# Two units of an attention, expert and gated chain with eight block products instead of seven

## The chip, the cores and the metric

One core of one Trainium2 chip runs the whole program. The metric is the device time of one execution in microseconds (us). TensorE (PE) does the matrix products and reads its stationary operand through a second row, PEld. VectorE (DVE), ScalarE (ACT) and GpSimd (POOL) do the elementwise work, SyncE (SP) issues the DMAs.

## The reference, cut to what matters

```python
x = attention(q, k, v)                   # 1152 tokens x 512
P = balanced_gates(x @ w_gate)           # 1152 x 8, eight rounds of scaling
out = sum(P[:, e:e+1] * (relu(x @ w1[e]) @ w2[e]) for e in range(8))   # 8 experts, 1024 wide
a, b = out @ w_a, out @ w_b              # 1536 wide
return (a * b) @ w_out
```

All of it is in float32, and the weights w_a, w_b and w_out come as 64-bit floats.

## The kernel before, in words

Each float32 operand is split into a high and a low part (ACT casts the high part, DVE or POOL subtracts it from the raw number for the low one, lines 130 to 140), and each product is done as three matmuls, high by high, high by low and low by high (lines 59, 60).

Half an expert (512 hidden columns) is a unit: units 0 and 1 are expert 0, unit 2 is the first half of expert 1, and so on to unit 15. After them come six gated units of 256 hidden columns each (`glu_g`), which multiply a by b instead of taking the maximum with zero. Units 0 and 1 run while the attention still runs, over blocks of 384 tokens.

From unit 2 on, the 1152 tokens are done in two chunks of 512 and 640 (`CN`, half a chunk is 256 or 320 tokens). Each of the two is a `phase`: the hidden layer of one unit and chunk (`g_chunk`), with the output tiles of the unit and chunk before (`o_tile`, 12 matmuls of 512 columns, 6 in a gated unit) put between its products at `PLACES`. The hidden layer is a product of 2 by 2 blocks, done with seven block products (A11, S2, S1, A12, S3, A22, S4) where eight are the plain way. Each block product is two groups of six matmuls. In return, sums have to be made: of weight blocks (`queue_combined`, seven blocks a unit, most of it on POOL) and of token blocks (`combine_x`: four totals on line 573, four differences on line 581, casts on line 587, low parts on line 594). The token sums T1 to T4 are made once for each chunk before unit 2, and again before the first gated unit, since there the tokens are the experts' output, transposed by `t_step`. T1 is written over a part of the tokens' own tiles `xh` and `xl`.

The program is written out in one order, and each engine keeps the order in which its instructions are emitted. What is emitted between the products is set by a small model of the engines' times (`Model`, `pump`, `force`): tasks stand in the queues `tq` (token sums), `wq` (weight splits) and `dq` (decoding of the 64-bit weights), and `pump` takes one when the model says that its engine has room. The decoding is 48 pieces through two buffers: load, an absolute value on ACT, seven instructions on DVE, an addition on POOL, and a store to DRAM (lines 330 to 402). What is left of it is run before unit 15 (lines 1319, 1320). PSUM gives six banks to hidden groups, and two to output tiles.

Steps of the change and of the prediction touch these lines: `queue_plain` 235, `queue_combined` 247, `combine_x` 541, `g_chunk` 616, `phase` 720, `close_attention` 1171, the end of units 0 and 1 at 1267 to 1278, unit 2 at 1304 to 1314, the first gated unit at 1331 to 1360.

Of the kernel before, what the change touches and what calls it, by code (L numbers as in the profile page):

```python
# [19 lines left out]
def attn_moe_glu_kernel(  # L20
# [16 lines left out]
    nc = tc.nc  # L37
# [21 lines left out]
    def mm(o, l, r, start, stop, check=True):  # L59
        nc.tensor.matmul(out=o, lhsT=l, rhs=r, start=start, stop=stop, skip_group_check=not check)  # L60
# [94 lines left out]
    def run(q):  # L155
        t = q.pop(0)
        t.fn()
        return t
# [14 lines left out]
    def force(cond):  # L173
        while not cond():
            if not (wq and (not wq[0].slot or slot_free() or RING[nring[0] % NSLOT].uses == 0)):
                raise RuntimeError("nothing left to prepare")
            run(wq)
# [54 lines left out]
        lq.extend(rs)  # L232
        return rs

    def queue_plain(u):

        u.w = {}
        rs = halves(u.load1, (2, 2))
        for i in range(2):
            for j in range(2):  # L240
                def piece(i=i, j=j):
                    b = u.w[i, j] = new_block(NB * 2)
# [373 lines left out]
    def g_chunk(u, c, glu=False):  # L616
# [44 lines left out]
        for a, b, bk in PRODUCTS:  # L661
# [46 lines left out]
                finish(0, 0, 0, G4[:, :n], True)  # L708
            yield


    PLACES = {5: (1, 2, 3, 4, 5), 4: (1, 3, 4, 5), 3: (1, 4, 5)}

# [5 lines left out]

    def phase(u, c, tiles, glu=False, places=None):  # L720

        places = places or PLACES[len(tiles)]
        for i, _ in enumerate(g_chunk(u, c, glu)):
            gate_step()
            for t, at in zip(tiles, places):
                if at == i:
                    t()
                    gate_step()
# [382 lines left out]
    with tc.manual_schedule():  # L1111
# [29 lines left out]
            queue_plain(u)  # L1141
        for u in units[:2]:
            queue_out(u)
        queue_combined(units[2], nc.gpsimd)
        extra = []

        def spare_block(uses):
# [21 lines left out]
                n -= run(wq).slot  # L1169

        def close_attention():
            nonlocal closed, ps3, Th, Tl, tmp_p
# [7 lines left out]
            tmp_p = tmp_stack.enter_context(tc.tile_pool(name="tmp", bufs=1, side="right"))  # L1180
            ps3 = ctx.enter_context(tc.tile_pool(name="ps3", bufs=6, space=PSUM))
            gens[0] = gating()
            v, g = nc.vector, nc.gpsimd
            tasks = combine_x(0, lambda name: tmp_p.tile([128, 2, CN[0]], F32, name=name),
                              (v, g, g, v), (g, g, g, g))
            tq.extend(tasks[:-2])
            late.extend(tasks[-2:])
            queue_out(units[2])
            for u in units[3:]:
                queue_combined(u)  # L1190
                queue_out(u)
            for u in glu_g:
                queue_combined(u)
                queue_out(u, 2)
            hold[0] = False
            for r in coming:
                r.tile
            fetch()
# [12 lines left out]
                else:  # L1211
                    close_attention()

        Th = Tl = tmp_p = G4 = None
        G3, late = [], []
        tmp_stack = ExitStack()
        turn = 0.0
        nside = 0

# [15 lines left out]
        for b in range(NB):  # L1235
            while ready[0] < b:
                side_step()
                if b == 0:
                    warm(WARM[1])
                nside += 1  # L1240
                if nside > 12 and nside % 2 == 0:
                    run_first(1)
            if b == NB - 1:
                while not closed:
                    side_step()
                M.dve = M.act = M.pe
# [8 lines left out]
            if b == NB - 1:  # L1255
                tq.extend(late)
            per = TB // 128
            firsts = [[
                lambda n=n, t=t, b=b: o_moe(
                    units[n], *([G[n][:, f] for f in range(4)] for G in GP), t, b * per + t, mid)  # L1260
                for t in range(per)
            ] for n in range(2)]
            for n in range(2 if b < NB - 1 else 1):
                for t in firsts[n]:
                    t()
                    step()
        while tq:
            run(tq)
        M.dve, M.act, M.pool = min(M.dve, M.pe + 1), min(M.act, M.pe + 1), min(M.pool, M.pe + 1)
        tmp_stack.close()  # L1270
        g0p = ctx.enter_context(tc.tile_pool(name="g0p", bufs=1, side="right"))
        t1 = {}
        for x, names in (("gh0", ("t1", "b12")), ("gl0", ("b22", "b21"))):
            t = gp.tile([128, 1536], F32, tag=x, name=f"t{x}")
            for i, name in enumerate(names):
                t1[name] = t[:, i * 640:(i + 1) * 640].rearrange("p (k n) -> p k n", k=2)
        v, g = nc.vector, nc.gpsimd
        tq.extend(combine_x(1, lambda name: t1[name], (v, g, g, v), (g, g, g, g)))
# [52 lines left out]
        def transposed(c, part=None):  # L1331
            x0, x1 = keep[c]
            where = {"t1": x0[:, 0:2], "b12": x1[:, 0:2], "b22": x1[:, 2:4], "b21": x0[:, 2:4]}
            tq.extend(combine_x(c, lambda name: where[name], (v, g, g, v), None, part))

        for t, tt in enumerate(TILES[1]):
            o_tile(units[last], 1, t)
            if t == 0:
                steps = [t_step(t0, keep) for t0 in TILES[0]]
                for _ in range(2):  # L1340
                    for x in steps:
                        next(x, None)
                transposed(0)
            else:
                for _ in t_step(TILES[1][t - 1], keep):
                    pass
                if t == 4:
                    transposed(1, slice(0, 192))
        while tq:
            run(tq)  # L1350
# [9 lines left out]
        phase(glu_g[0], 1, o_tiles(glu_g[0], 0), True)  # L1360
# [35 lines left out]
```

## Time and profile before

| What | us |
|---|---|
| three runs, median | 1136.14 |
| lowest and highest of the three | 1133.69, 1141.28 |
| the profiled execution | 1141.77 |
| its span, from the first to the last instruction | 1140.0 |

The profiled execution lies 5.6 us above the median. Its mean granted clock is 0.974. Times of rows are counted from the start of the span. PEclk is the granted clock of TensorE as a share of 2.4 GHz (1.00 in text), 0.50 is 1.2 GHz.

### The profile page before, as it was taken

Reading aid. Unit: us, or ns where it says so; the run is one execution under the profiler, and the core shown is the slowest. Engines: PE = TensorE matmul, PEld = TensorE weight load, DVE = VectorE, ACT = ScalarE, POOL = GpSimd, SP = SyncE. Lnnn points to the kernel's source line nnn. Section 1 sums busy time; section 2 is a strip of 40 time slices with the busy share of each in tenths; the row PEclk is TensorE's granted clock in tenths of the full one; section 3 lists DMA queues with packets and bytes.
Section 4 is the critical chain, followed back from the end, with each engine's and each line's share of the span. In section 5 each row is a group of like instructions: output and inputs, shape, how many; then the busy total and the mean of one; then the engine's idle time right before and its main releaser. Section 6 shows DMA issues by size and latency. Waiting matters only on the chain.

```text
span 1140.0 us, 18222 instructions
## 1 busy us (share of the span) xinstructions
PE 1097.3 (96%) x6545; PEld 994.1 (87%) x6545; DVE 804.1 (71%) x1593; ACT 459.0 (40%) x1203; POOL 541.6 (48%) x540
## 2 busy tenths in 40 slices
PE   8998999979999999999999999999999979999998
PEld 6897898768889999899998999989899778999997
DVE  6566453777878878778787788877754665666764
ACT  5555442344344443444434444344443532323321
POOL 3312312475355464554645646456453334546431
PEclk9599999989999999999999999999999989999999
DMA  6243200112322323323233132331310101011102
GB/s 168 52 130 101 65 16 1 38 66 65 100 97 75 118 71 120 99 66 118 85 114 97 62 118 84 114 97 61 109 54 22 38 19 37 20 56 56 56 20 83
DMA packets 80841, 84.51 MB, mean 74 GB/s; under 512 B 35952, under 2 KB 54384, under 8 KB 80752
## 3 DMA queue, kind: packets, MB, share of 16 engines
q1 hardware_dynamic: 80752, 83.36, 23.9%
q8 instruction: 51, 0.84, 0.3%
q14 instruction: 38, 0.31, 0.1%
HBM read 71.54 MB, written 11.80 MB: 73 GB/s over the span
## 4 chain that ended last, share of the span: by engine, by line
PE 88%; DVE 6%; ACT 2%; POOL 2%; issue 1%; DMA 0%; DVEq 0%; SPq 0%; POOLq 0%; ACTq 0%
PE g L60 82%; PE at L60 4%; DVE w L135 1%; DVE G L647 1%; ACT p L905 1%; PE at L936 1%; ACT Th L587 0%; DVE xt L581 0%; DVE tgh L581 0%; POOL vd L821 0%; POOL tgh L573 0%; DVE G L657 0%; PE g L734 0%; POOL p L920 0%; PE at L833 0%
## 5 line engine op out<-in xcount | busy, mean ns | idle before, releaser
L60 PE MATMUL g<-w,gh 128*128 128x512 f32 x1314 | 412.6, 395 | 3.9 <-DVE acc L508 1.8
L60 PE MATMUL g<-xh,w 128*128 128x256 f32 (+2 forms) x1472 | 329.9, 305 | 4.5 <-ACT G L683 3.3
L643 POOL TENSOR_TENSOR gl<-G,gh 128x256 fp32r<-128x256 f32 (+1 forms) x216 | 182.5, 853 | 276.6 <-ACT gh L641 265.4
L60 PEld LDWEIGHTS g<-w,gh 128*128 128x128 f32 x1314 | 237.8, 190 | 44.3 <-DVE acc L508 2.0
L60 PE MATMUL g<-w,gl 128*128 128x512 f32 x657 | 258.9, 394 | 0.0
L60 PEld LDWEIGHTS g<-xh,w 128*128 128x128 f32 x1472 | 249.5, 191 | 9.9 <-ACT G L683 3.5
L60 PE MATMUL g<-Th,w 128*128 128x256 f32 (+1 forms) x960 | 214.5, 300 | 14.3 <-DVE G L647 7.0
L60 PE MATMUL g<-xl,w 128*128 128x256 f32 (+2 forms) x736 | 223.3, 303 | 0.5 <-POOL xl L978 0.5
L135 DVE TENSOR_TENSOR w<-raw,w 128x512 fp32r<-128x512 f32 x138 | 134.8, 984 | 106.4 <-ACT w L134 106.4
L647 DVE TENSOR_TENSOR G<-g,G 128x256 f32<-128x256 f32 (+1 forms) x400 | 164.6, 449 | 34.7 <-PE g L60 23.0
L60 PEld LDWEIGHTS g<-Th,w 128*128 128x128 f32 x960 | 164.3, 193 | 19.8 <-DVE G L647 8.3
L639 ACT ACTIVATE G<-G 128x256 f32<-128x256 f32 (+1 forms) x168 | 74.4, 443 | 215.9 <-DVE G L647 215.2
L60 PEld LDWEIGHTS g<-w,gl 128*128 128x128 f32 x657 | 124.4, 189 | 27.1
L60 PEld LDWEIGHTS g<-xl,w 128*128 128x128 f32 x736 | 140.5, 191 | 5.1 <-POOL xl L978 1.0
L60 PE MATMUL g<-Tl,w 128*128 128x256 f32 (+1 forms) x480 | 143.6, 299 | 0.3 <-DVE Tl L594 0.3
L641 ACT CAST gh<-G 128x256 fp32r<-128x256 f32 (+1 forms) x216 | 93.6, 433 | 108.5 <-DVE G L657 91.6
L134 ACT CAST w<-raw 128x512 fp32r<-128x512 f32 x181 | 108.2, 619 | 40.1 <-POOL raw L259 36.5
L508 DVE SCALAR_TENSOR_TENSOR acc<-g,P,acc 128x512 f32<-128x512 f32 x126 | 93.7, 744 | 30.0 <-PE g L60 28.7
L60 PEld LDWEIGHTS g<-Tl,w 128*128 128x128 f32 x480 | 92.3, 192 | 3.8 <-DVE Tl L594 0.7
L389 POOL TENSOR_TENSOR dec<-dec 128x384 f32<-128x384 f32 x48 | 49.8, 1037 | 76.1 <-DVE dec L386 65.7
L259 POOL TENSOR_TENSOR raw<-raw 128x512 f32<-128x512 f32 x40 | 54.5, 1363 | 42.0 <-DVE w L135 25.5
L259 POOL TENSOR_TENSOR s<-raw 128x512 f32<-128x512 f32 x40 | 65.6, 1640 | 1.0 <-DMA raw<-w 0.7
(171 smaller groups left out, 1209.6 us busy)
## 6 DMA issues: line engine op xcount, KB each, us to landing
raw<-in_moe_w_dram SPq DMA_DIRECT2D x128, 256.0 KB
w<-dec SPq DMA_DIRECT2D x48, 192.0 KB
dec<-in_moe_w_a_dram SPq DMA_DIRECT2D x16, 384.0 KB
dec<-in_moe_w_b_dram SPq DMA_DIRECT2D x16, 384.0 KB
dec<-in_moe_w_out_dram SPq DMA_DIRECT2D x16, 384.0 KB
raw<-w SPq DMA_DIRECT2D x48, 128.0 KB
raw<-w SPq DMA_DIRECT2D x12, 256.0 KB
vw<-in_v_dram SPq DMA_DIRECT2D x72, 35.0 KB
```

Source lines behind the costliest of these rows:

```text
L60: nc.tensor.matmul(out=o, lhsT=l, rhs=r, start=start, stop=stop, skip_group_check=not check)
L134: nc.scalar.copy(out=hi, in_=raw)
L135: (low or nc.vector).tensor_tensor(out=lo, in0=raw, in1=hi.bitcast(F32), op=ALU.subtract)
L259: nc.gpsimd.tensor_tensor(out=o(), in0=A(*a), in1=A(*b), op=op)
L389: nc.gpsimd.tensor_tensor(out=tf, in0=tf, in1=mf, op=ALU.add)
L508: nc.vector.scalar_tensor_tensor(out=a, in0=ps, scalar=P[:, tt, u.e:u.e + 1], in1=a, op0=ALU.mult, op1=ALU.add)
L639: nc.scalar.activation(out=src, in_=src, func=AF.Relu)
L641: nc.scalar.copy(out=h, in_=src)
L643: nc.gpsimd.tensor_tensor(out=l, in0=src, in1=h.bitcast(F32), op=ALU.subtract)
L647: nc.vector.tensor_tensor(out=o, in0=bank_, in1=b, op=ALU.add)
L905: nc.scalar.activation(out=p[:, c], in_=sl[:, c * W:(c + 1) * W], func=AF.Exp, bias=nm[:, c:c + 1], scale=1.0, accum_out=rs[:, c:c + 1],)
L936: nc.tensor.transpose(pt[0:W, c * 128:(c + 1) * 128], p[:, c], ident)
```

## The change

Unit 2 and the first gated unit take their weight blocks plain (four of them, `queue_plain`) and do eight block products in a new function `g_whole`, in eight groups of twelve matmuls a chunk, each with its own bank. The token sums are made during these two units and not before them: of the first chunk while unit 2 does the first chunk, of the second while it does the second. Their temporary tiles for the second chunk are the decoding's two buffers, so the decoding is queued after the first phase of unit 3 and not before the second phase of unit 2. At the gated unit the totals come from `t_step` as before, and the sums are queued in full length after the last token tile.

```diff
-    def queue_plain(u):
+    def queue_plain(u, uses=6):
...
+    def g_whole(u, c, glu=False):
+        n = CN[c]
...
+        for i in range(2):
+            force(lambda: (i, 1) in u.w)
+            for j in range(2):
+                cols = HALF[c][j]
+                for fi in range(2):
+                    p = bank("g")[:, :n]
+                    k = 0
+                    for kt in range(KT):
+                        w = u.w[i, kt // 2]
+                        o = (kt % 2) * 256 + fi * 128
+                        a_h, a_l = w.hi[:, o:o + 128], w.lo[:, o:o + 128]
+                        for lt, rt in ((a_h, xh), (a_h, xl), (a_l, xh)):
+                            mm(p, lt, rt[:, kt, cols], k == 0, k == 3 * KT - 1)
+                            k += 1
...
+                    pump()
+                    f = i if glu else i * 2 + fi
+                    sl = slice(j * n, (j + 1) * n)
+                    h, l = GH[c][f][:, sl], GL[c][f][:, sl]
+                    t = G3[i][j][:, :n]
+                    if not glu:
+                        nc.scalar.activation(out=h, in_=p, func=AF.Relu)
+                        nc.vector.scalar_tensor_tensor(
+                            out=l, in0=p, scalar=0.0, in1=h.bitcast(F32), op0=ALU.max, op1=ALU.subtract
+                        )
+                    elif fi == 0:
+                        nc.scalar.copy(out=t, in_=p)
+                    else:
+                        nc.vector.tensor_tensor(out=t, in0=p, in1=t, op=ALU.mult)
+                        nc.scalar.copy(out=h, in_=t)
+                        nc.gpsimd.tensor_tensor(out=l, in0=t, in1=h.bitcast(F32), op=ALU.subtract)
+                yield
...
-        places = places or PLACES[len(tiles)]
-        for i, _ in enumerate(g_chunk(u, c, glu)):
+        whole = hasattr(u, "w")
+        places = places or ((0, 1, 2, 2, 3)[5 - len(tiles):] if whole else PLACES[len(tiles)])
+        for i, _ in enumerate((g_whole if whole else g_chunk)(u, c, glu)):
...
-        queue_combined(units[2], nc.gpsimd)
+        queue_plain(units[2], 8)
...
-            tasks = combine_x(0, lambda name: tmp_p.tile([128, 2, CN[0]], F32, name=name),
-                              (v, g, g, v), (g, g, g, g))
...
             for u in glu_g:
-                queue_combined(u)
+                if u is glu_g[0]:
+                    queue_plain(u, 8)
+                else:
+                    queue_combined(u)
                 queue_out(u, 2)
...
-        firsts[1][0]()
-        phase(units[2], 0, firsts[1][1:], False, (1, 4))
+        rest = sums(0, [gp.tile([128, 1536], F32, tag=x, name=f"t{x}") for x in ("gh0", "gl0")])
+        phase(units[2], 0, firsts[1], False, (0, 1, 2))
         while tq:
             run(tq)
+        for t in rest:
+            run([t])
...
-        queue_decode()
-        ahead[0] = 1.0
+        rest = sums(1, [spare_tile(i, F32, f"t{i}") for i in range(2)])
         last = len(units) - 1
         phase(units[2], 1, o_tiles(units[2], 0))
+        tq.extend(rest)
         for i in range(3, last):
             phase(units[i], 0, o_tiles(units[i - 1], 1))
+            if i == 3:
+                while tq:
+                    run(tq)
+                queue_decode()
+                ahead[0] = 1.0
             phase(units[i], 1, o_tiles(units[i], 0))
...
-                if t == 4:
-                    transposed(1, slice(0, 192))
-        while tq:
-            run(tq)
...
-            transposed(1, slice(192, 320))
+            transposed(1)
 
         phase(glu_g[0], 0, [last_step], True, (0,))
+        tq[:0] = late[:2]
+        phase(glu_g[0], 1, o_tiles(glu_g[0], 0), True)
+        tq.extend(late[2:])
         while tq:
             run(tq)
```

`sums` calls `combine_x` with the totals on POOL and puts all its tasks but the last two (T1, written over the tokens) into `tq`; the last two are `rest`.

The first place is DVE where unit 2 begins, right after the last step of the gates (P, ct). Before, t, b and tgh, tgl hold token sums, w_2775 and w_2778 are output weights of unit 2, G its kept sums:

```order
L1042 SCALAR_TENSOR_TENSOR P<-P,ct 128x9x8
L581 TENSOR_TENSOR t_2477<-b_2479,t_2477 128x512
L581 TENSOR_TENSOR b_2479<-b_2481,b_2479 128x512
L581 TENSOR_TENSOR b_2481<-b_2481,t_2477 128x512
L581 TENSOR_TENSOR b_2502<-b_2502,b_2481 128x512
L594 TENSOR_TENSOR Tl<-b_2481,Th 128x2x256
L594 TENSOR_TENSOR xl<-t_2477,xh 128x2x256
L135 TENSOR_TENSOR w_2775<-raw,w_2775 128x512
L135 TENSOR_TENSOR w_2778<-raw,w_2778 128x512
L504 TENSOR_TENSOR acc_87<-g_2759,acc_87 128x512
L581 TENSOR_TENSOR tgh_2753<-tgh_2753 128x640
L581 TENSOR_TENSOR tgh_2753<-tgl_2754,tgh_2753 128x640
```

In the changed program the same place reads as follows; w_2702 and w_2705 are the first two weight blocks of unit 2, gl its hidden layer's low part:

```order
L1090 SCALAR_TENSOR_TENSOR P<-P,ct 128x9x8
L135 TENSOR_TENSOR w_2702<-raw,w_2702 128x512
L135 TENSOR_TENSOR w_2705<-raw,w_2705 128x512
L742 SCALAR_TENSOR_TENSOR gl_2698<-g_2708,gh_2696 128x256
L581 TENSOR_TENSOR tgh_2700<-tgh_2700 128x512
L742 SCALAR_TENSOR_TENSOR gl_2698<-g_2726,gh_2696 128x256
L581 TENSOR_TENSOR tgh_2700<-tgl_2701,tgh_2700 128x512
L581 TENSOR_TENSOR tgl_2701<-tgl_2701,tgh_2700 128x512
L581 TENSOR_TENSOR tgl_2701<-tgl_2701 128x512
L504 TENSOR_TENSOR acc_87<-g_2743,acc_87 128x512
```

The sums went behind the first groups of unit 2, and the splits of its first weight blocks, which POOL did earlier, now stand on DVE behind the gates.

The second place is ACT where unit 15 begins: G_2443 and G_2444 are unit 14's last kept sums, g_8829 and g_8836 the first two groups of unit 15, dec_8605, dec_8787 and dec_8807 the last three pieces of the decoding. In the changed program:

```order
L346 ACTIVATE dec_8605<-dec_8605 128x384
L639 ACTIVATE G_2443<-G_2443 128x320
L641 CAST gh_2916<-G_2443 128x320
L639 ACTIVATE G_2444<-G_2444 128x320
L641 CAST gh_2916<-G_2444 128x320
L346 ACTIVATE dec_8787<-dec_8787 128x384
L346 ACTIVATE dec_8807<-dec_8807 128x384
L683 COPY G_2441<-g_8829 128x256
L683 COPY G_2442<-g_8836 128x256
```

Before, ACT has none of the decoding there (g_8858 and g_8865 are unit 15's first two groups):

```order
L639 ACTIVATE G_2447<-G_2447 128x320
L641 CAST gh_2966<-G_2447 128x320
L134 CAST w_8872<-s_8826 128x512
L683 COPY G_2444<-g_8858 128x256
L683 COPY G_2445<-g_8865 128x256
```

DVE has the seven instructions of each of these three pieces in one block at the same place, 21 instructions ahead of its first work for unit 15.

The third place is DVE at the first gated unit, behind the low parts of the last token tiles. Before, every sum that the first products need stands ahead of the unit's own additions (G, line 647); xh, xl and xt are here the temporary tiles of the sums where no g stands on the right:

```order
L594 TENSOR_TENSOR Tl<-xl,Th 128x2x256
L594 TENSOR_TENSOR xl<-xh 128x2x256
L581 TENSOR_TENSOR xt_9295<-xt_9296,xt_9295 128x2x192
L581 TENSOR_TENSOR xt_9296<-xt_9296 128x2x192
L581 TENSOR_TENSOR xt_9296<-xt_9296,xt_9295 128x2x192
L581 TENSOR_TENSOR xt_9295<-xt_9295,xt_9296 128x2x192
L594 TENSOR_TENSOR Tl<-xt_9296,Th 128x2x192
L594 TENSOR_TENSOR xl<-xt_9295,xh 128x2x192
L739 TENSOR_TENSOR xl<-g_9475,xh 128x4x128
L647 TENSOR_TENSOR G_2446<-g_9483,G_2444 128x256
```

In the changed program they stand between the multiplications a by b (line 750):

```order
L750 TENSOR_TENSOR G_2441<-g_9420,G_2441 128x256
L787 TENSOR_TENSOR xl<-g_9439,xh 128x4x128
L581 TENSOR_TENSOR xh<-xh,xl 128x512
L594 TENSOR_TENSOR Tl<-xl,Th 128x2x256
L135 TENSOR_TENSOR w_9479<-raw,w_9479 128x512
L750 TENSOR_TENSOR G_2442<-g_9464,G_2442 128x256
L581 TENSOR_TENSOR xt_9267<-xt_9268,xt_9267 128x640
L581 TENSOR_TENSOR xt_9268<-xt_9268 128x640
L581 TENSOR_TENSOR xt_9268<-xt_9268,xt_9267 128x640
L750 TENSOR_TENSOR G_2443<-g_9501,G_2443 128x256
```

The multiplications wait in DVE's queue behind sums, where before the additions waited behind all of them.

## Rows read from the trace of the kernel before

**Rows 1.** Page, part 1: busy time, share of the span, instructions.
```profile
PE 1097.3 (96%) x6545; PEld 994.1 (87%) x6545; DVE 804.1 (71%) x1593; ACT 459.0 (40%) x1203; POOL 541.6 (48%) x540
```

**Rows 2.** Windows: stretch, length, busy us (instructions) by engine, PEclk, DMA share, GB/s.
```profile
222.84:275.18 52.34, 45.02 (x253) 40.17 (x253) 44.26 (x63) 21.48 (x48) 33.67 (x25) 0.93 0.21 67
275.18:293.58 18.40, 16.03 (x87) 13.56 (x86) 13.32 (x30) 6.20 (x15) 5.63 (x6) 0.91 0.22 73
293.58:892.98 599.40, 599.40 (x3518) 543.03 (x3516) 463.91 (x826) 257.90 (x597) 328.07 (x303) 1.00 0.27 88
907.46:950.52 43.06, 33.84 (x199) 31.21 (x198) 29.32 (x53) 13.95 (x32) 15.06 (x15) 0.88 0.05 13
950.52:958.85 8.33, 5.60 (x30) 4.95 (x29) 3.58 (x7) 3.59 (x8) 6.84 (x6) 0.80 0.00 0
958.85:1136.00 177.15, 177.10 (x1114) 163.98 (x1112) 117.35 (x210) 47.57 (x107) 80.01 (x74) 1.00 0.16 50
...
239.00:241.00 2.00, 1.29 (x6) 1.29 (x7) 2.00 (x5) 1.60 (x3) 0.21 (x1) 0.50 0.00 0
```

**Rows 3.** Timeline of PE: start, us, instruction, count, [idle before it and releaser].
```profile
239.71 0.58 PE L60 MATMUL g<-Th,w 128*128 128x256 f32 x1 [5.03 <-DVE G L647]
...
289.14 0.83 PE L60 MATMUL g<-w,gh 128*128 128x512 f32 x2 [1.82 <-DVE acc L508]
...
919.15 0.58 PE L60 MATMUL g<-xh,w 128*128 128x256 f32 x1 [3.28 <-ACT G L683]
```

**Rows 4.** Timeline of PE: first matmuls of groups that follow each other without a gap.
```profile
226.06 0.28 PE L60 MATMUL g<-xh,w 128*128 128x256 f32 x1
...
227.49 0.29 PE L60 MATMUL g<-Th,w 128*128 128x256 f32 x1
...
254.72 0.62 PE L60 MATMUL g<-w,gh 128*128 128x512 f32 x2
...
257.48 0.31 PE L60 MATMUL g<-xh,w 128*128 128x320 f32 x1
...
261.01 0.63 PE L60 MATMUL g<-w,gh 128*128 128x512 f32 x2
```

**Rows 5.** Waits of PE from 190 to 226 us: us, times, longest.
```profile
PE g L60 <- DVE P L1030: 1.6, 3, 0.7
```

**Rows 6.** Timelines of ACT, DVE and POOL around the start of unit 2.
```profile
222.68 0.58 ACT L498 COPY acc<-g 128x512 f32<-128x512 f32 x1 [2.96 <-PE g L60]
...
225.31 0.69 DVE L581 TENSOR_TENSOR b<-b,t 128x512 f32<-128x512 f32 x1
...
229.03 3.76 DVE L135 TENSOR_TENSOR w<-raw,w 128x512 fp32r<-128x512 f32 x2
...
188.93 1.26 POOL L573 TENSOR_TENSOR t<-xh,xl 128x512 f32<-128x512 f32 x1 [0.28 <-PE at L60]
...
230.22 3.99 POOL L573 TENSOR_TENSOR tgh<-xh,xl 128x640 f32<-128x640 f32 x2
```

**Rows 7.** Page, part 5: groups by line with busy us, mean ns of one, idle before.
```profile
L647 DVE TENSOR_TENSOR G<-g,G 128x256 f32<-128x256 f32 (+1 forms) x400 | 164.6, 449 | 34.7 <-PE g L60 23.0
...
L134 ACT CAST w<-raw 128x512 fp32r<-128x512 f32 x181 | 108.2, 619 | 40.1 <-POOL raw L259 36.5
...
L508 DVE SCALAR_TENSOR_TENSOR acc<-g,P,acc 128x512 f32<-128x512 f32 x126 | 93.7, 744 | 30.0 <-PE g L60 28.7
```

**Rows 8.** Windows of the tile dec alone: DVE, ACT, POOL busy us (instructions), PEclk, DMA.
```profile
257.00:817.00 560.00, 203.10 (x336) 26.71 (x48) 49.76 (x48) 1.00 0.29 94
```

**Rows 9.** Timeline of SP: a store of a decoded piece and the next load.
```profile
269.46 0.33 SPq L390 DMA_DIRECT2D w<-dec  x1
271.38 0.33 SPq L335 DMA_DIRECT2D dec<-in_moe_w_a_dram  x1
```

**Rows 10.** Window 2.62 us after that load's issue, as in rows 2.
```profile
274.00:274.50 0.50, 0.50 (x6) 0.50 (x5) 0.50 (x2) 0.00 (x0) 0.00 (x0) 1.00 0.00 0
```

**Rows 11.** Waits of ACT over the span: us, times, longest.
```profile
ACT dec L346 <- DMA dec<-in_moe_w_out_dram: 18.1, 4, 5.2
```

More of the change, by code (lines that the diff above doesn't have):

```diff
@@ L241, in piece @@
                 def piece(i=i, j=j):
-                    b = u.w[i, j] = new_block(NB * 2)
+                    b = u.w[i, j] = new_block(uses)
                     split(b, rs[j].tile[:, :, 256 * i:256 * i + 256], 2)
@@ L709, in g_chunk @@
             yield
+    def g_whole(u, c, glu=False):
+        n = CN[c]
+        us = n / 960 + 0.165
+        aus = n / 1200 + 0.17
+        pus = n / 460 + 0.23
+        for i in range(2):
[12 more added lines that the diff above has]
+                            k += 1
+                    M.pe += 12 * (n / 2400 + 0.0135)
+                    for x in range(2):
+                        u.w[i, x].use()
+                    pump()
[5 more added lines that the diff above has]
+                        nc.scalar.activation(out=h, in_=p, func=AF.Relu)
+                        act(aus)
+                        nc.vector.scalar_tensor_tensor(
+                            out=l, in0=p, scalar=0.0, in1=h.bitcast(F32), op0=ALU.max, op1=ALU.subtract
+                        )
+                        dve(us)
+                    elif fi == 0:
+                        nc.scalar.copy(out=t, in_=p)
+                        act(aus)
+                    else:
+                        nc.vector.tensor_tensor(out=t, in0=p, in1=t, op=ALU.mult)
+                        dve(us)
+                        nc.scalar.copy(out=h, in_=t)
+                        act(aus)
+                        nc.gpsimd.tensor_tensor(out=l, in0=t, in1=h.bitcast(F32), op=ALU.subtract)
+                        pool(pus)
+                yield
     PLACES = {5: (1, 2, 3, 4, 5), 4: (1, 3, 4, 5), 3: (1, 4, 5)}
@@ L1171, in close_attention @@
         def close_attention():
-            nonlocal closed, ps3, Th, Tl, tmp_p
+            nonlocal closed, ps3, Th, Tl
             closed = True
@@ L1179, in close_attention @@
                 G3.append([tp.tile([128, 320], F32, name=f"G{x}{fi}") for fi in range(2)])
-            tmp_p = tmp_stack.enter_context(tc.tile_pool(name="tmp", bufs=1, side="right"))
             ps3 = ctx.enter_context(tc.tile_pool(name="ps3", bufs=6, space=PSUM))
             gens[0] = gating()
-            v, g = nc.vector, nc.gpsimd
-            tasks = combine_x(0, lambda name: tmp_p.tile([128, 2, CN[0]], F32, name=name),
-                              (v, g, g, v), (g, g, g, g))
-            tq.extend(tasks[:-2])
-            late.extend(tasks[-2:])
             queue_out(units[2])
@@ L1212, in side_step @@
                     close_attention()
-        Th = Tl = tmp_p = G4 = None
+        Th = Tl = G4 = None
         G3, late = [], []
-        tmp_stack = ExitStack()
         turn = 0.0
@@ L1254, in attn_moe_glu_kernel @@
                 run_first(1)
-            if b == NB - 1:
-                tq.extend(late)
             per = TB // 128
@@ L1266, in attn_moe_glu_kernel, with sums @@
                     step()
-        while tq:
-            run(tq)
-        M.dve, M.act, M.pool = min(M.dve, M.pe + 1), min(M.act, M.pe + 1), min(M.pool, M.pe + 1)
-        tmp_stack.close()
         g0p = ctx.enter_context(tc.tile_pool(name="g0p", bufs=1, side="right"))
[L1272 to L1276, printed above, removed]
-        v, g = nc.vector, nc.gpsimd
-        tq.extend(combine_x(1, lambda name: t1[name], (v, g, g, v), (g, g, g, g)))
+        v, g = nc.vector, nc.gpsimd
+        def sums(c, tiles):
+            n = 2 * CN[c]
+            where = {}
+            for t, names in zip(tiles, (("t1", "b12"), ("b22", "b21"))):
+                for i, name in enumerate(names):
+                    where[name] = t[:, i * n:(i + 1) * n].rearrange("p (k n) -> p k n", k=2)
+            tasks = combine_x(c, lambda name: where[name], (v, g, g, v), (g, g, g, g))
+            tq.extend(tasks[:-2])
+            return tasks[-2:]
         GH, GL = [], []
@@ L1329, in attn_moe_glu_kernel, with transposed @@
         ]
-        def transposed(c, part=None):
+        def transposed(c):
             x0, x1 = keep[c]
             where = {"t1": x0[:, 0:2], "b12": x1[:, 0:2], "b22": x1[:, 2:4], "b21": x0[:, 2:4]}
-            tq.extend(combine_x(c, lambda name: where[name], (v, g, g, v), None, part))
+            tasks = combine_x(c, lambda name: where[name], (v, g, g, v), None)
+            tasks[0].ready = lambda t=M.pe: M.pe >= t + 3.0
+            tq.extend(tasks[:-2])
+            late.extend(tasks[-2:])
+        late.clear()
         for t, tt in enumerate(TILES[1]):
@@ L1346, in attn_moe_glu_kernel @@
                     pass
-                if t == 4:
-                    transposed(1, slice(0, 192))
-        while tq:
-            run(tq)
         def last_step():
@@ L1354, in last_step @@
                 pass
-            transposed(1, slice(192, 320))
+            transposed(1)
         phase(glu_g[0], 0, [last_step], True, (0,))
+        tq[:0] = late[:2]
+        phase(glu_g[0], 1, o_tiles(glu_g[0], 0), True)
+        tq.extend(late[2:])
         while tq:
             run(tq)
-        phase(glu_g[0], 1, o_tiles(glu_g[0], 0), True)
         for g_ in range(1, GU):
```

## The prediction

> **What bounds the kernel now.** Page part 1 first: TensorE is busy 96% of the span [rows 1], so a change pays only where it has PE do less, or where PE stands still. The windows by stage say where that is [rows 2]. From 293.58 to 892.98 us PE is busy all of the 599.40 us at clock 1.00, and from 958.85 on 177.10 of 177.15; an engine that is late there costs nothing. PE loses time at the two places where token sums are made and first used: around unit 2 (first and second row) and around the first gated unit (fourth and fifth). PE's timeline names the causes [rows 3]: 5.03 us before the first product of unit 2 that reads a token sum (Th), released by DVE, 1.82 at unit 3 on DVE's additions to acc, and 3.28 in the gated unit. Behind such a gap the clock is down: it is 0.50, the 1.2 GHz level, in 239 to 241 us [rows 2], right behind the 5.03.
>
> What the products need without stalls comes from the starts of groups that follow without a gap [rows 4]: 227.49 − 226.06 is 1.43 for twelve matmuls of 256 columns, 0.119 each; 257.48 to 261.01 is 3.53 for 24 of 320 columns, 0.147 each; 254.72 to 257.48 is 2.76 for an output tile of twelve (1.38 for the six of a gated unit).
>
> **The change part by part**, as gain (−) or cost (+) in us against the profiled execution, 1141.77.
>
> *Products.* One block product more per chunk is 12 × 0.119 + 12 × 0.147 = 3.2 us a unit, and two units do it: +6.4, all on PE. It is charged in the parts below.
>
> The Trainium skill ("TensorE: Matmul & The Clock Gate", section Back-to-back issue gap) has a sustained 81 ns for 128 columns and 131 ns for 512; between them that makes an estimated 98 and 106 ns here, and 4.9 instead of 6.4. The trace has 230 ns at 512 (2.76/12), so the measurement decides.
>
> *Ahead of unit 2.* PE waits three times, 1.6 us in all, for P, the gates' table, while DVE and POOL also make token sums [rows 5]. The sums move away: **−1.6** (bounds −1.6 and 0).
>
> *Unit 2.* It takes 52.34 us, from 222.84 to 275.18 [rows 2]. Its matmuls need 84 × 0.119 + 84 × 0.147 + 7 × 2.76 = 41.7, so 10.7 is lost. Afterwards they need 44.8. The wait for Th goes, since no product reads a sum. What is late next is the first weight: its two low parts (w) now stand on DVE right behind the gates (first place of the order), where before POOL made them during units 0 and 1. ACT's last copy of units 0 and 1 ends at 222.68 + 0.58 = 223.26 [rows 6]; a cast of 0.62 [rows 7] makes the high part at 223.9. DVE's subtraction of that size takes 0.69 where POOL is idle (a token sum of the same 128x512) and 3.76/2 = 1.88 where POOL works [rows 6]. POOL makes the totals there, so I take 1.88: the weights stand at 225.8 and 227.6, the first group (1.43) ends between them, and PE idles about 3.9. With 0.69 it is 1.5. The clock then is low for a first group or two; half speed costs one group's time per group, 1.43 each, and I take 2 (0 to 2.8). So 44.8 + 3.9 + 2 is 50.7, or **−1.5**. Bounds: −6.0 (1.5, no clock) to 0 (2.8 for the clock, 0.7 for a bank late).
>
> *Start of unit 3.* 18.40 us for 4 × 1.43 + 3 × 2.76 = 14.0 [rows 2, 4], so 4.4 lost, 1.82 of it on acc [rows 3]. The decoding is no longer there; but the second chunk's sums are, up to the end of unit 3's first phase. I take 2.0 of stall left, **−2.4** (−4.4 to 0).
>
> *Start of unit 15.* The decoding is queued behind unit 3's first phase and no longer ahead of unit 2's second, a phase of each chunk later; it worked from 257 to 817 [rows 8], and unit 15 begins near 845, so what was to spare is used up. So three pieces are run off at one go (second place of the order), and SP, ACT, DVE and POOL are each in order. From PE's start of unit 15: DVE's seven instructions of a piece are 203.10/48 = 4.23 [rows 8], from +0.9 on, so +5.1; POOL's addition 49.76/48 = 1.04, +6.2; on SP the store at 269.46 and the next load at 271.38 stand 1.92 apart [rows 9]; the load has landed 2.62 after its issue, when the DMA share is 0 [rows 10], so +10.7; ACT's absolute value 26.71/48 = 0.56, +11.3; and behind it in ACT's queue two copies of unit 15's groups, +11.9. PE by then has 3 × 1.43 + 2 × 2.76 = 9.8 us of work: about 2 idle. DVE's last piece ends near +15, two additions (0.45 each) and acc (0.74) [rows 7] follow, and an output bank for PE comes near +16.5, 3 late. 4.5 to 6 idle, plus 1 to 2 for the clock: **+6.5**. Lower bound 0: ACT waited up to 5.2 on such a load before, four times [rows 11], and PE lost nothing in that stretch [rows 2]. Upper bound: all three pieces one after the other through store, load, ACT, DVE and POOL, 1.92 + 2.62 + 0.56 + 4.23 + 1.04 = 10.4 each, 31.1 less PE's 9.8 is 21.3, plus 2 for the clock, 23.
>
> *First gated unit.* 43.06 us, where its matmuls need 84 × 0.119 + 84 × 0.147, four output tiles and 0.35 of transposes, 28.2: 14.9 lost, with PEclk 0.88 [rows 2]. Behind it 8.33 for 24 × 0.119 and half a tile, 3.55: 4.8 lost. In all 19.7. Afterwards the first chunk's eight groups read plain tokens, 11.4 us of work; the sums of the first chunk stand between the multiplications (third place of the order) and are next needed by the second gated unit, some 30 us on. By the order, the six banks come free in time: the ninth group (at +11.4) needs a bank that ACT and DVE read by +5, and the one at +17.1 a multiplication that is due by +15. I leave 1.0 of stall. −19.7 + 3.2 + 1.0 = **−15.5**. Bounds: −16.5, and −8.7 as worked out under contention below.
>
> Sum: −1.6 − 1.5 − 2.4 + 6.5 − 15.5 = −14.5, that is 1127.3 beside the profiled 1141.77. This execution lies 5.6 above the median, as its whole, so I take the difference off the median: 1136.14 − 14.5 = **1121.6**.
>
> **The rivals.**
>
> *Quick:* the tail at unit 15 is hidden, as decoding waits were before [rows 11], and unit 2's first weight comes early (1.5, no clock). −1.6 − 6.0 − 2.4 + 0 − 15.5 is −25.5; with 1 to 2 kept for the clock −24: **1112**. Against it: the third piece shares a buffer with the first, so its load cannot start before the first is stored.
>
> *Contention at the gated unit:* DVE has 16 subtractions and sums of two SBUF operands within the unit's 31.3 us while POOL has the totals and the low parts. If each takes 1.88 and not 0.69 [rows 6], that is 16 × 1.19 = 19.0 more on top of about 19 of DVE's work (29.32 [rows 2] less some 23 additions of 0.449 [rows 7]): 38.1, 6.8 more than PE's 31.3. Multiplications wait behind them, banks with these. The part is then −8.7, the whole −7.7: about **1128**, within 1%. For it: the pairs at 229.03 and 230.22 run slow together. Against: not all of POOL's work lies beside them, and 52.34 us of unit 2 hold 44.26 of DVE without a stop of that size.
>
> On this the Trainium skill ("SBUF — State Buffer", section Who interferes with whom) says that a DVE instruction with two SBUF inputs and a GpSimd one lock each other out of a shared port wholly. Here 0.69 and POOL's 1.26 alone [rows 6] add up to 1.95, and 1.88 a piece was measured beside POOL, so the trace agrees; by that rule every such pair is serial, which is this rival at its full price.
>
> *Slower, the decoding's tail:* the three pieces run in series as in the upper bound, 23 at unit 15, PE standing with them, against 21.0 gained elsewhere: +2, **1138**. From a loss of 21.0 at unit 15 on, the change no longer pays; over 1% slower needs 32, beyond that bound. For it: one buffer pair and in-order queues. Against: two buffers let two pieces overlap, and DVE's part is 12.7 of it.
>
> **How the numbers follow.** Forecast 0.52, quick 0.16, contention 0.24, decoding's tail 0.08. About 1% is what a measurement of this kernel can tell from no change: faster below 1124.8, slower above 1147.5. The forecast's own range, 1116 to 1128, lies some 0.83 below 1124.8 (0.43), quick wholly (0.16), contention at a tenth (0.02): faster 0.61. The slower rival at its end and what I have not thought of make 0.05, and the rest, 0.34, is the same. The range 1109 to 1134 leaves out the far half of the slower rival and the ends of the others.
>
> **What would show it.** In the changed profile: no wait for P ahead of unit 2; about 4 us of PE idle at its first group, released by DVE's w, and the clock down behind it; some 2 at unit 3; 4 to 6 at unit 15, released by ACT's copies and by acc; and next to none in the first gated unit, its windows near 31 and 4 us at clock 1.00. I am wrong if the gated unit still idles above 5 us (contention), if unit 15 loses over 21, or if PE stalls in units 3 to 14, where I count nothing.

## The result, and the profile after

The changed kernel takes 1127.1 us, the median of 13 runs (1120.6 to 1132.7), against 1136.1 before (13 runs, 1130.4 to 1142.8). The ratio is 0.9909, with a 95% interval of 0.988 to 0.9938: faster by 7 to 14 us, 10.3 at the ratio itself. The forecast was 14.5 faster, 1121.6. The prediction had set its own mark for "faster" at 1124.8, and 1127.1 lies above it: in its terms this is "the same", to which it gave 0.34, where it gave 0.61 to faster. With 13 runs of each the interval does tell the gain from none.

The profiled execution took 1130.06 us (span 1128.3), 2.9 above its median, where the one of before lay 5.6 above its own. The busy times of page part 1, which answer to [rows 1], hardly move for TensorE:

```profile
PE 1095.5 (97%) x6593; PEld 994.4 (88%) x6593; DVE 799.1 (71%) x1564; ACT 449.4 (40%) x1179; POOL 508.4 (45%) x507
```

The 48 matmuls more are 4 block products more of 12. What changed is where PE stands, and the windows by stage show that, with the columns of [rows 2]. The first is unit 2, then the start of unit 3, the units up to the first tiles of unit 15, the stand in unit 15, the rest up to the gated unit, the gated unit, and the start of the second one:

```profile
219.73:271.54 51.81, 48.66 (x277) 43.95 (x278) 39.06 (x49) 18.29 (x38) 31.48 (x19) 0.93 0.15 46
271.54:285.43 13.89, 13.89 (x86) 12.43 (x84) 7.24 (x14) 2.55 (x6) 0.00 (x0) 1.00 0.27 97
285.43:846.80 561.37, 560.73 (x3289) 506.57 (x3287) 449.60 (x796) 239.94 (x555) 309.03 (x285) 1.00 0.29 93
846.80:862.10 15.30, 7.18 (x25) 6.05 (x26) 9.10 (x20) 2.91 (x7) 3.22 (x3) 0.67 0.25 86
862.10:912.34 50.24, 50.24 (x285) 44.53 (x284) 28.96 (x49) 24.39 (x53) 12.59 (x14) 1.00 0.19 53
912.34:943.98 31.64, 31.64 (x224) 30.60 (x223) 20.67 (x28) 16.06 (x34) 22.35 (x17) 1.00 0.07 23
943.98:952.00 8.02, 8.02 (x58) 7.52 (x57) 6.86 (x10) 2.90 (x7) 4.70 (x4) 1.00 0.39 113
```

The gated unit, 43.06 us before, takes 31.64 with PE busy to the last hundredth and the clock at 1.00, and the second one starts without a gap. Unit 3's start takes 13.89 where it took 18.40. Unit 2 is hardly shorter. And there is a new hole: 15.30 us in unit 15 for a group and an output tile that need 1.43 + 2.76, with PE busy for 7.18 and the clock at 0.67. PE's timeline names who it waited for, in unit 2 (the first four rows) and in unit 15:

```profile
219.73 0.39 PE L60 MATMUL g<-xh,w 128*128 128x256 f32 x1 [1.00 <-ACT w L134]
...
221.49 0.51 PE L60 MATMUL g<-xh,w 128*128 128x256 f32 x2 [1.25 <-DVE w L135]
...
223.18 0.80 PE L60 MATMUL g<-xh,w 128*128 128x256 f32 x2 [0.71 <-DVE w L135]
...
262.38 0.74 PE L60 MATMUL g<-w,gh 128*128 128x512 f32 x2 [1.19 <-DVE acc L508]
...
853.15 0.58 PE L60 MATMUL g<-xh,w 128*128 128x256 f32 x1 [6.36 <-ACT G L683]
...
857.85 1.22 PE L60 MATMUL g<-w,gh 128*128 128x512 f32 x2 [1.77 <-DVE acc L508]
```

**How to compare two profiles of this kernel.** The two spans differ by more than the stages do, since each execution has its own start. The first 60 us tell how. This is the row of the kernel before,

```profile
0.00:60.00 60.00, 53.32 (x346) 48.29 (x346) 35.29 (x127) 31.96 (x134) 22.63 (x45) 0.77 0.43 110
```

and this one that of a run below (decoding late) whose program is the same up to unit 2:

```profile
0.00:60.00 60.00, 51.82 (x393) 46.17 (x393) 39.39 (x141) 35.92 (x148) 24.37 (x47) 0.94 0.52 130
```

The granted clock is 0.77 in one and 0.94 in the other, 47 matmuls more are done by then, and the last product of the gates (PE, g from P) starts at 222.49 and at 213.18. So I count from that product on, by the starts of matmuls in PE's timeline, and split the rest at places that every kernel here has: unit 3's first matmul, the eighth stretch of products behind it (a stretch is a run of products of one kind, up to the next change of kind), unit 5's first product, unit 15's first product, and the first transposition at the gated unit.

| us | to unit 3 | unit 3's start | on to unit 5 | to unit 15 | unit 15 | gated units to the end | sum |
|---|---|---|---|---|---|---|---|
| before | 52.8 | 19.7 | 78.7 | 469.7 | 49.6 | 247.0 | 917.5 |
| after | 53.2 | 15.3 | 80.5 | 469.7 | 60.9 | 230.4 | 909.9 |
| gated unit alone | 52.8 | 18.1 | 79.6 | 469.9 | 49.6 | 230.5 | 900.5 |
| unit 2 alone | 51.7 | 15.3 | 79.4 | 469.7 | 59.9 | 247.2 | 923.3 |
| decoding late | 52.2 | 15.2 | 80.6 | 469.9 | 62.1 | 248.1 | 928.1 |
| rest spread | 51.9 | 15.3 | 80.2 | 469.7 | 49.6 | 230.3 | 897.0 |
| five a unit | 51.9 | 15.3 | 80.7 | 475.6 | 49.8 | 230.1 | 903.4 |
| sums first | 51.9 | 15.3 | 80.3 | 471.0 | 49.6 | 231.4 | 899.5 |
| splits on POOL | 49.7 | 15.3 | 80.0 | 469.7 | 49.6 | 230.3 | 894.6 |

Where nothing was touched the columns agree between kernels to about 1.5 us (unit 3's start, 19.7 and 18.1 in the first and third row, is the worst of them). Three numbers make the result: −16.6 in the last stage, −2.8 to −4.4 at unit 3, and +11.3 at unit 15. A smaller one, +0.9 to +1.8, comes between unit 3's start and unit 5.

### The profile page after: what moved, and what is told of

It reads as the page before. It is cut to its first block, busy times and chain, and to the rows that moved or that the text cites. A ratio compares the mean times of both kernels' runs of the same rounds, so it can differ in the third digit from the quotient of the medians.

```text
span 1128.3 us, 18202 instructions
## 1 busy us (share of the span) xinstructions
PE 1095.5 (97%) x6593; PEld 994.4 (88%) x6593; DVE 799.1 (71%) x1564; ACT 449.4 (40%) x1179; POOL 508.4 (45%) x507
## 4 chain that ended last, share of the span: by engine, by line
PE 86%; DVE 6%; ACT 3%; POOL 2%; DMA 2%; issue 2%; SPq 0%; DVEq 0%; ACTq 0%; POOLq 0%
PE g L60 79%; PE at L60 4%; DVE w L135 1%; ACT w L134 1%; DVE acc L508 1%; ACT p L953 1%; PE at L984 1%; DMA raw<-in_moe_w_dram 1%; DVE G L647 0%; DMA dec<-in_moe_w_a_dram 0%; POOL gl L643 0%; DVE t L581 0%; POOL vd L869 0%; PE g L782 0%; ACT G L639 0%
## 5 line engine op out<-in xcount | busy, mean ns | idle before, releaser
L60 PE MATMUL g<-xh,w 128*128 128x320 f32 (+2 forms) x1600 | 357.5, 305 | 10.1 <-ACT G L683 6.4
L643 POOL TENSOR_TENSOR gl<-G,gh 128x256 fp32r<-128x256 f32 (+1 forms) x196 | 166.3, 857 | 271.6 <-ACT gh L641 258.8
L60 PEld LDWEIGHTS g<-xh,w 128*128 128x128 f32 x1600 | 271.7, 192 | 16.4 <-ACT G L683 6.8
L60 PE MATMUL g<-xl,w 128*128 128x320 f32 (+2 forms) x800 | 243.1, 304 | 0.5 <-POOL xl L1026 0.5
L60 PE MATMUL g<-Th,w 128*128 128x256 f32 (+1 forms) x864 | 188.7, 295 | 0.1
L647 DVE TENSOR_TENSOR G<-g,G 128x256 f32<-128x256 f32 (+1 forms) x360 | 148.1, 449 | 21.4 <-PE g L60 12.3
L60 PEld LDWEIGHTS g<-xl,w 128*128 128x128 f32 x800 | 153.3, 192 | 4.9 <-POOL xl L1026 1.0
L60 PEld LDWEIGHTS g<-Th,w 128*128 128x128 f32 x864 | 144.5, 189 | 4.2 <-DVE G L647 1.6
L60 PE MATMUL g<-Tl,w 128*128 128x256 f32 (+1 forms) x432 | 127.2, 295 | 0.0
L60 PEld LDWEIGHTS g<-Tl,w 128*128 128x128 f32 x432 | 81.2, 188 | 2.8
```

The source lines that it names most:

```text
L643: nc.gpsimd.tensor_tensor(out=l, in0=src, in1=h.bitcast(F32), op=ALU.subtract)
L647: nc.vector.tensor_tensor(out=o, in0=bank_, in1=b, op=ALU.add)
```

## The experiments

**The gated unit alone.** The kernel before with the gated half of the change (`g_whole`, plain weights for the first gated unit, its sums behind it); unit 2, its sums and the place of the decoding stay.

```diff
...
             for u in glu_g:
-                queue_combined(u)
+                if u is glu_g[0]:
+                    queue_plain(u, 8)
+                else:
+                    queue_combined(u)
...
         phase(glu_g[0], 0, [last_step], True, (0,))
+        tq[:0] = late[:2]
+        phase(glu_g[0], 1, o_tiles(glu_g[0], 0), True)
+        tq.extend(late[2:])
         while tq:
             run(tq)
-        phase(glu_g[0], 1, o_tiles(glu_g[0], 0), True)
```

> Only the first gated unit has its eight block products; unit 2, its sums and the place of the decoding stay as before. Theory (the parts add up): the gated unit takes 31.6 us instead of 43.1 and the second one loses its 4.8 at the start, so 1136.1 - 16.6 = 1119.5, ratio 0.985, and PE does not stand at unit 15. Rival (a later start of the decoding is not what costs at unit 15): PE stands there as in the changed kernel, and the time is about that of the changed kernel, 1127, ratio 0.992.

1121.0 us, ratio 0.9857 (0.9812 to 0.9901): the theory. The windows of the gated unit and of the next 8 us are those of the changed kernel to 0.01 us, and unit 15 costs its old 49.6:

```profile
900.53:932.17 31.64, 31.64 (x224) 30.60 (x223) 20.72 (x28) 16.22 (x35) 22.31 (x17) 1.00 0.07 21
932.17:940.20 8.03, 8.03 (x58) 7.52 (x57) 6.83 (x10) 2.75 (x7) 4.71 (x4) 1.00 0.41 118
```

By the table this half gives −17.0 where the whole change gives −7.6, and the rival, that PE would stand at unit 15 in any case, is out.

**Unit 2 alone.** The other half: plain weights and eight products in unit 2, its sums behind it, the decoding after unit 3's first phase.

```diff
...
-        queue_combined(units[2], nc.gpsimd)
+        queue_plain(units[2], 8)
...
-        queue_decode()
-        ahead[0] = 1.0
+        rest = sums(1, [spare_tile(i, F32, f"t{i}") for i in range(2)])
         last = len(units) - 1
         phase(units[2], 1, o_tiles(units[2], 0))
+        tq.extend(rest)
         for i in range(3, last):
             phase(units[i], 0, o_tiles(units[i - 1], 1))
+            if i == 3:
+                while tq:
+                    run(tq)
+                queue_decode()
+                ahead[0] = 1.0
             phase(units[i], 1, o_tiles(units[i], 0))
```

> Only unit 2 has its eight block products, with its sums behind them and the decoding queued after unit 3's first phase; the gated units are as before. Theory: -3.1 ahead of unit 2, -0.5 in it, -4.4 at unit 3, +1.3 in units 3 and 4, +11.3 at unit 15 add up to +4.6: 1140.7, ratio 1.004, so this half of the change makes the kernel slower. Rival (the gain ahead of unit 2 is scatter between executions): +7.7, 1143.8, ratio 1.007. By the steps of the prediction it would be +1.0, 1137.

1143.7, ratio 1.0052 (1.0018 to 1.0085): this half alone makes the kernel slower. The interval holds both readings of the 3 us ahead of unit 2. The table speaks for scatter: it has +5.8 from the gates on, which is all of the 0.52% measured, and the same program reached that point 9 us apart above. Of the 5.8, −1.1 is unit 2, −4.4 unit 3's start, +0.7 the way to unit 5, +10.3 unit 15, the rest the gated units. The window of its unit 15, 49.6 us before:

```profile
838.56:898.50 59.94, 51.34 (x289) 45.77 (x288) 36.69 (x67) 21.90 (x52) 28.62 (x27) 0.94 0.21 62
```

**Decoding late.** The disputed cost by itself: the kernel before, with the decoding queued where the changed kernel has it.

```diff
-        queue_decode()
-        ahead[0] = 1.0
         last = len(units) - 1
         phase(units[2], 1, o_tiles(units[2], 0))
         for i in range(3, last):
             phase(units[i], 0, o_tiles(units[i - 1], 1))
+            if i == 3:
+                queue_decode()
+                ahead[0] = 1.0
             phase(units[i], 1, o_tiles(units[i], 0))
```

> The kernel before with one edit: the decoding is queued after unit 3's first phase, as in the changed kernel; nothing else. Theory: three pieces are left at unit 15 and PE loses about 11.3 us there, nothing elsewhere: 1147.4, ratio 1.010. Rival (the stand at unit 15 comes from the changed kernel's weights or banks): no change, 1136.

1145.9, ratio 1.0084 (1.0053 to 1.0116), +9.6: the stand is the decoding's, with the same releasers as in the changed kernel and none of its weights:

```profile
847.82 0.58 PE L60 MATMUL g<-xh,w 128*128 128x256 f32 x1 [6.88 <-ACT G L683]
...
852.73 1.22 PE L60 MATMUL g<-w,gh 128*128 128x512 f32 x2 [1.98 <-DVE acc L508]
```

"Nothing elsewhere" was wrong, and that is the second finding. Unit 3's start fell from 19.7 (18.1 in the run of the gated unit alone) to 15.2, though the token sums were left where they had been:

```profile
265.43:279.50 14.07, 14.07 (x88) 12.61 (x87) 5.84 (x13) 3.60 (x9) 1.74 (x2) 1.00 0.12 38
```

DVE is busy 5.84 of these 14.07 us, against 13.32 of 18.40 in [rows 2]. What stood on DVE there before was the decoding, not the sums. The window of the tile dec alone in the kernel before (DVE, ACT, POOL, as in [rows 8]) has 6.53 us of it, and no token sum (line 581) or low part of one (line 594) falls into that stretch:

```profile
275.18:293.58 18.40, 6.53 (x16) 1.10 (x2) 2.14 (x2) 0.91 0.22 73
```

**The rest spread.** The changed kernel, where the three pieces left are not run ahead of unit 15 but taken up during its two phases.

```diff
-        while dq:
-            run(dq)
         phase(units[last], 0, o_tiles(units[last - 1], 1))
         phase(units[last], 1, o_tiles(units[last], 0))
+        while dq:
+            run(dq)
```

> The changed kernel with one edit: what is left of the decoding is not run ahead of unit 15 but taken up piece by piece during its two phases. Theory: the 11.3 us at unit 15 go, 1127.1 - 11.3 = 1115.8, ratio to before 0.982. Rival (the pieces cost PE the same wherever they stand, since DVE and the DMA have no room): 1123 to 1127, ratio 0.989 to 0.992, with the idle time in unit 15 or at the gated unit's first weights.

1115.6, ratio 0.9806 (0.975 to 0.9862), which beats both kernels. The whole of unit 15, which had the hole, runs without one:

```profile
835.96:885.56 49.60, 49.60 (x290) 44.65 (x288) 38.29 (x70) 21.54 (x51) 21.15 (x23) 1.00 0.35 107
```

DVE does 38.29 us of work in it, and PE waits for nothing. The windows of dec alone show that unit 15 holds as much of the decoding here (first row) as in the changed kernel (second row), so it was the block that cost, not the pieces:

```profile
835.96:885.56 49.60, 12.29 (x23) 1.57 (x3) 4.07 (x4) 1.00 0.35 107
...
837.02:897.88 60.86, 12.30 (x23) 1.56 (x3) 4.02 (x4) 0.92 0.29 87
```

**Five a unit.** The same aim by another way: the decoding goes faster in units 12 to 14.

```diff
                 ahead[0] = 1.0
+            if i == last - 3:
+                ahead[0] = 1.5
             phase(units[i], 1, o_tiles(units[i], 0))
```

> The changed kernel with one edit: in the last three units of the loop the decoding takes five pieces a unit instead of four, so that nothing is left at unit 15. Theory: the 11.3 us at unit 15 go as they did when the rest was spread over unit 15: 1116, ratio to before 0.981. Rival (DVE, the DMA and SP have no room for a fifth piece a unit): PE stands in units 12 to 14 for part of it, 1119 to 1127, ratio 0.985 to 0.992.

1119.4, ratio 0.984 (0.9799 to 0.9881), at the near end of the rival's range. Unit 15 is whole (49.8), but 5.9 us are lost ahead of it. The window of one such place has DVE busy for 15.63 of 16.00:

```profile
770.00:786.00 16.00, 14.04 (x75) 12.18 (x74) 15.63 (x26) 4.57 (x10) 8.39 (x7) 1.00 0.33 107
```

and DVE's timeline there has the decoding's one-operand steps at several times their 0.36 us, beside two POOL additions (776.84, 3.10 for two):

```profile
777.35 1.45 DVE L352 TENSOR_SCALAR dec<-dec 128x384 f32<-128x384 f32 x1
778.83 1.33 DVE L357 TENSOR_SCALAR dec<-dec 128x384 int32<-128x384 int32 x1
```

So DVE has no room for a fifth piece at these places, and PE pays for it. The interval does not part this kernel from the one with the rest spread (0.975 to 0.9862); the profiles do, 903.4 against 897.0.

**Sums first.** The kernel with the rest spread, where the first chunk's sums at the gated unit are run ahead of its products, as before the change; the products stay plain.

```diff
+        while tq:
+            run(tq)
         phase(glu_g[0], 0, [last_step], True, (0,))
```

> The kernel with the decoding's rest spread over unit 15, and one more edit: the first chunk's sums stand ahead of the first gated unit's products in the queues, as in the kernel before, but the products stay the eight plain ones. Theory (the gain of the gated unit comes from products that read no sums; DVE has room): the unit keeps its 31.6 us or loses at most 2: 1115.6 to 1117.6, ratio 0.982 to 0.984. Rival (the gain comes from where the sums stand): the multiplications come late, the banks with them, and 5 us or more are lost: 1121, ratio 0.987.

1115.4, ratio 0.9793 (0.9748 to 0.9839). The unit takes 32.63 instead of 31.64, with one wait of 0.72 on an output tile:

```profile
897.21:929.84 32.63, 31.91 (x224) 30.52 (x222) 20.03 (x29) 16.69 (x35) 20.84 (x17) 1.00 0.11 33
```

The gain at the gated unit comes from products that read no sums; where the sums stand is worth 1.0 us in this profile.

**Splits on POOL.** The kernel with the rest spread, where POOL and not DVE makes the low parts of unit 2's weights, ahead of its totals.

```diff
-                    split(b, rs[j].tile[:, :, 256 * i:256 * i + 256], 2)
+                    split(b, rs[j].tile[:, :, 256 * i:256 * i + 256], 2, low)
                     rs[j].used()
-                wq.append(Task(piece, 0.68, ready=rs[j].ready, slot=True))
+                wq.append(Task(piece, 0.0 if low else 0.68, 1.35 if low else 0.0, ready=rs[j].ready, slot=True))
...
-        queue_plain(units[2], 8)
+        queue_plain(units[2], 8, nc.gpsimd)
```

> The kernel with the decoding's rest spread over unit 15, and one more edit: the low parts of unit 2's four weight blocks are made on POOL, ahead of its token totals and during the gates. Theory: the 1.0 + 1.3 + 0.7 us of PE's idle time at unit 2's first group go, and with them most of the 2.7 at the low clock behind it: 1115.6 - 5 = 1110.6, ratio to before 0.977. Rival (DVE's steps of the gates and POOL's four subtractions slow each other, and the totals come four subtractions later): the waits for P come back, 1.6, and acc is late in unit 2: 1114 to 1116, ratio 0.981.

1114.3, ratio 0.9798 (0.9752 to 0.9844): no difference from the rest spread that the times can tell. The profile shows 2.4 of the 5 us. PE's idle time at unit 2's first group is gone, and part of it comes back in the two ways that the rival named, as waits for P and as a later acc:

```profile
200.23 0.46 PE L60 MATMUL g<-P,ones 128*128 128x90 f32 x2 [0.44 <-DVE P L1078]
...
203.67 0.43 PE L60 MATMUL g<-P,ones 128*128 128x90 f32 x2 [0.86 <-DVE P L1078]
...
257.49 0.51 PE L60 MATMUL g<-w,gh 128*128 128x512 f32 x1 [2.66 <-DVE acc L508]
```

DVE's product of P and ct, 0.23 us alone, took 1.19 beside POOL's splits:

```profile
198.20 1.19 DVE L1090 SCALAR_TENSOR_TENSOR P<-P,ct 128x72 f32<-128x72 f32 x1
```

## Why the prediction was right, and by how much it was off

It was right in sign, in its shape (a large gain at the gated unit, a smaller one at units 2 and 3, a cost at unit 15) and in its range. Its middle was 4.2 us too low by the ratio and 5.5 by the medians, mainly for one term.

*Products and the gated unit, −15.5.* Right: −16.6 in the table, 31.64 us with no stall where 32.4 had been allowed, and the second gated unit's 4.8 gone.

*Contention there (rival).* Not the case, though the effect is real. In the changed kernel's gated unit DVE's timeline has the same sort of subtraction at 0.69 and, beside POOL, at 1.80:

```profile
918.73 0.69 DVE L594 TENSOR_TENSOR Tl<-xl,Th 128x512 fp32r<-128x512 f32 x1
...
923.77 1.80 DVE L581 TENSOR_TENSOR xt<-xt,xt 128x640 f32<-128x640 f32 x1
...
930.03 0.69 DVE L594 TENSOR_TENSOR xl<-xh 128x512 fp32r<-128x512 f32 x1 [0.99 <-ACT xh L587]
```

(the 128x640 one takes 0.81 alone, at 921.64). The rival counted 16 such operations at their full price, 38 us of DVE; the unit has 20.67. Of the 14 in DVE's timeline there, six took longer than alone, 4.5 us in all; the totals there come from `t_step` and not from POOL. PE waits for nothing in the unit, so the 4.5 found room between 20.67 and 31.64. The rival had given about 1128 for the whole, and 1127.1 was measured: that its number came nearer than the forecast's is chance, since its step did not happen. The Trainium skill ("SBUF — State Buffer", section Who interferes with whom) says the two engines exclude each other for a DVE instruction with two SBUF inputs beside a GpSimd one that reads SBUF, and for a tensor_scalar in a mode that uses both ports; the 1.80 here and the 1.45 for a tensor_scalar of 0.36 above agree, though no run shows the tensor_scalar's mode. The rule gives the price of a pair, not whether the engine had time to pay it.

*Waits for P, −1.6.* They are gone from the changed kernel's waits. The time to that point scatters by more, so no run shows the 1.6 as time.

*Unit 2, −1.5* (1.6 by its own figures, 52.34 − 50.7). Right to within the scatter, and no more: 52.8, or 52.2 in one run, became 51.7 to 53.2, so it gained 1.1 at most, and the changed kernel's own row in the table, 53.2, shows no gain. By its steps: PE idles 1.00 + 1.25 + 0.71 = 3.0 at the first group where 3.9 was said, released by w as said; the two splits took 3.41 for two, 1.7 each, beside POOL's totals. Then comes 1.19 on acc between the two phases, which the sum did not have.

*Unit 3, −2.4.* The gain was larger, −2.8 to −4.4 (15.2 or 15.3 in all seven kernels that start the decoding later, 18.1 and 19.7 in the two that do not), and its step was wrong: I left 2 us to the second chunk's sums, but the decoding had made the stall, as the run with only the decoding moved shows, and of the sums only one low part (line 594, 0.81 us) still fell into this stretch of the changed kernel. In exchange up to 2 us came on the way to unit 5, in units 3 and 4, where the decoding now starts (80.0 to 80.7 in six of these, 79.4 in one, against 78.7 and 79.6). I had counted nothing in units 3 to 14; PE stands there for 0.64 us of the changed kernel's 561.37, 0.39 of it on acc.

*Unit 15, +6.5.* This is the term that failed, by size: 11.3 (10.3 and 12.5 in the two runs that isolate it). The mechanism was as told: three pieces at one go, ACT's copies of the hidden groups behind the last absolute value, acc behind the last piece. ACT's timeline:

```profile
848.51 0.55 ACT L346 ACTIVATE dec<-dec 128x384 f32<-128x384 f32 x1 [6.26 <-DMA dec<-in_moe_w_out_dram]
852.29 0.54 ACT L346 ACTIVATE dec<-dec 128x384 f32<-128x384 f32 x1 [3.24 <-DMA dec<-in_moe_w_out_dram]
852.74 0.63 ACT L683 COPY G<-g 128x256 f32<-128x256 f32 x2
```

Unit 15 begins at 837.02, so PE goes on at +16.1, where the copies had been put at +11.9. DVE's and SP's timelines say why:

```profile
838.60 0.78 DVE L382 TENSOR_SCALAR dec<-dec 128x384 int32<-128x384 int32 x1
839.42 0.56 DVE L386 SCALAR_TENSOR_TENSOR dec<-dec 128x384 f32<-128x384 int32 x1
839.89 0.88 DVE L647 TENSOR_TENSOR G<-g,G 128x320 f32<-128x320 f32 x2
840.69 0.60 DVE L352 TENSOR_SCALAR dec<-dec 128x384 f32<-128x384 f32 x1
...
844.82 0.56 DVE L386 SCALAR_TENSOR_TENSOR dec<-dec 128x384 f32<-128x384 int32 x1
```

```profile
839.19 1.75 SPq L409 DMA_DIRECT2D raw<-in_moe_w_dram  x4
841.11 0.33 SPq L390 DMA_DIRECT2D w<-dec  x1
845.48 0.33 SPq L335 DMA_DIRECT2D dec<-in_moe_w_out_dram  x1
846.49 0.33 SPq L390 DMA_DIRECT2D w<-dec  x1
849.17 0.33 SPq L335 DMA_DIRECT2D dec<-in_moe_w_out_dram  x1
```

The first of the forced pieces ended on DVE at 845.4, +8.4 and not +5.1: a weight's subtraction, an addition to acc, the end of the piece before it and two additions to G stood in front, which I had not counted, so it began at +3.7 and not +0.9 (2.8), and it took 4.69 and not 4.23 (0.5); 3.3 together. From its store to the next load it was 2.68 and not 1.92 (0.8), and from that load's issue to ACT 3.12 and not 2.62 (0.5). Together that is 4.6, a little more than the 4.2 between +11.9 and +16.1. The stand of 6.36 is then 16.1 less PE's 9.8, and 1.77 on acc follows; the clock, 0.80 in the window from 850 to 851 us and 0.50 in the one from 851, takes the other 3: the group and the output tile there needed 2.94 and 4.25 us instead of 1.43 and 2.76, where 1 to 2 had been allowed.

```profile
850.00:851.00 1.00, 0.00 (x0) 0.00 (x0) 0.96 (x3) 0.00 (x0) 0.00 (x0) 0.80 0.82 209
851.00:852.00 1.00, 0.00 (x0) 0.00 (x0) 0.93 (x3) 0.00 (x0) 0.00 (x0) 0.50 0.47 184
```

*The slower rival* was the same chain at 23 us; 11.3 lies less than a third of the way from the forecast's 6.5 to it. The quick one (tail hidden) is out for this change; the run with the rest spread is that case at unit 15, though not at unit 2, and its 1115.6 lies 3.6 above the 1112 given for it.

*The sum.* −16.6, some −3.6 at unit 3, −1 at unit 2, +1 on to unit 5 and +11.3 make −8.9, and −10.5 with the waits for P; measured −10.3 (−7 to −14). The middle values at units 2, 3 and 5 are taken over all runs; the two profiles alone have −7.6 from the gates on. Beside unit 15's 4.8 the other differences from the forecast are small and nearly cancel: −1.1 at the gated unit, −1.2 at unit 3, +0.5 at unit 2 and +1 on to unit 5.

What stays open: why the first 60 us are granted so different a clock in runs of the same program, and what of unit 2's last 5 us (acc between its phases, the clock) could still be had. Also open is what unit 2's eight products are worth by themselves. The run with the rest spread is 3.5 us ahead of the gated unit alone in the table (897.0 against 900.5), of which unit 3's start, which the decoding makes, is 2.8 and unit 2 itself 0.9; no run has unit 2's seven products with the decoding late and its rest spread.

## What to carry to other kernels

A step that is moved takes with it whatever is started behind it: here a gain of 3 to 5 us at units 2 and 3, most of it made by the decoding's leaving, was paid for with a decoding that began later and ended as one block ahead of in-order engines, 11 us. Background work with no slack left was best spread over the last stage that it may run in, where DVE still had room (38.29 of 49.60), and not run off at one go ahead of it; a faster pace for it costs where the engine that does it is full (15.63 of 16.00). Before a stall is put down to one of two neighbours, move one of them alone.

## What was not expected of the hardware

The granted clock of the first 60 us was 0.69 to 0.94 in the nine profiles here, and the last product of the gates started between 213.2 and 222.5 us in programs that are the same, or nearly, up to there. That is as wide as the scatter of ±6 us between runs; that it makes that scatter is likely, but not shown run by run. A store of 192 KB and the load into the same buffer stood 1.92 us apart in [rows 9], where the DMA share between the two was 0.29; in the changed kernel they stood 2.68 apart at a share of 0.62, with the other buffer's load of 384 KB on its way, and 4.37 apart (841.11 to 845.48) at 0.73, with four weight loads of 256 KB issued just ahead.
